# Chunk attention and a multiplicative FFN on one core: the first q and k through the software queue, another order of steps, and three PSUM tiles for the last output

## The chip, the cores and the metric

The kernel runs on one core of one Trainium2 chip. The metric is the device time of one execution in microseconds. The median of four executions before the change is 254.48 us (254.33 to 254.82).

## What is computed

Attention within chunks of 64 positions, then a feed-forward part without a nonlinearity, cut to the core:

```
B, H, S, D = 8, 8, 576, 64            # 9 chunks of 64 in each batch
scores = (q_c @ k_c^T) / sqrt(D)      # 64 x 64 for each chunk and head
attn   = exp(scores - max) / sum
x      = (attn @ v_c), heads side by side      # 4608 tokens x 512
out    = ((x @ w1) * (x @ w2)) @ w3 @ w_out    # w1, w2: 512 x 1024; w3: 1024 x 1024; w_out: 1024 x 512
```

The inputs and the output are fp32.

## The kernel before

The 4608 tokens are cut into 18 "pairs" of 256 tokens, four chunks each. The kernel works in bf16 with sums in fp32. It uses that w3 and w_out follow each other without a nonlinearity: it computes their product once, on the chip, so each pair needs x @ w1, x @ w2, their product, and one further matmul.

All work is written as small steps, and the string ORDER (lines 9 to 37) lists them one after the other. Every instruction is recorded so that each engine keeps this program order. A step that comes earlier in the string therefore stands ahead of all later ones in the queue of its engine, and an engine whose next instruction has to wait stands still. The steps, with p a pair:

- l p loads q, k and v of a pair, q p, k p and v p one of them. i n loads a quarter of the columns of w1 and w2, o loads w_out, h0 and h1 the halves of w3. These loads are issued by GpSimd (POOL) on its software queue and turn fp32 into bf16 on the way (line 91). A load of q or k of a pair writes 1024 rows of 256 bytes; where a pair crosses from one batch into the next, it is split in two. v is loaded in two halves, with rows of 128 bytes.
- q and k of pair 0 are the exception (lines 128 to 134): SP loads them as fp32 into a tile named raw, and ScalarE turns them into bf16.
- T p.0 and T p.1 (VectorE, line 168) transpose q and k in 32x32 blocks. S (TensorE) computes the scores, E (ScalarE, line 184) the exponential, P (TensorE) the product with v, which has a column of ones for the sum. N p.u (VectorE, lines 207 and 209) divides by the sum, X p.u (line 213) transposes the result into xt.
- A p.j and B p.j (TensorE, line 231) multiply xt with quarter j of w1 and of w2. C (ScalarE, line 244) copies A's result out of PSUM, M (VectorE, line 249) multiplies it with B's result into the tile ab.
- V f (VectorE, line 290) transposes an eighth of w3. W m (TensorE) multiplies with w_out, and Z m (ScalarE, line 303) stores that into w3o.
- O p (TensorE, line 260) multiplies ab with w3o, Y p (ScalarE, line 283) copies the result out, and SP stores it. O of the last pair, 17, does this in three parts: first 128 tokens with all 512 columns, then the other 128 tokens with 256 columns and with 256 columns. Each part is copied out (line 276; ScalarE, ScalarE, VectorE) and stored at once.
- D p multiplies zeros, only to keep TensorE busy at the start. Its four numbers are the kind of PSUM tile, the pair, how many, and the columns of each.

All matmuls share one pool of four PSUM tiles of two banks each (lines 81 and 94); a new tile takes the place of the fourth one before it, once that has been read. P takes two tiles. Index u of the tile, or which for A and B, selects the bank.

The 18 pairs are staggered. From pair 5 on, a "slot" takes the attention of a new pair between the matmuls of older pairs: S and P of the new pairs, one O, and the four A and B of another pair.

Of the kernel before, what the change touches and what calls it, by code (L numbers as in the profile page):

```python
# [7 lines left out]

ORDER = """
l0 q1 i0 k1 v1 i1 i2 l2 i3 l3 l4 o h0 h1 l5 D0.0.16.64 T0.0 T0.1 l6 S0 T1.0 E0 P0 D0.1.4.512 T1.1 l7  # L10
N0.0 S1 D1.0.5.512 X0.0 N0.1 X0.1 A0.0 E1 B0.0 C0.0 P1 M0.0 A0.1 N1.0 X1.0 B0.1 C0.1 N1.1 A0.2 X1.1
B0.2 C0.2 M0.1 A1.0 T2.0 B1.0 C1.0 M0.2 A1.1 T2.1 l8 B1.1 C1.1 M1.0 S2 M1.1 A0.3 E2 T3.0 B0.3 C0.3
P2 M0.3 A1.2 N2.0 X2.0 B1.2 C1.2 N2.1 A1.3 X2.1 B1.3 C1.3 M1.2 A2.0 T3.1 l9 B2.0 C2.0 M1.3 S3 T4.0
A2.1 E3 M2.0 B2.1 T4.1 C2.1 P3 l10 M2.1 A2.2 N3.0 B2.2 C2.2 X3.0 A2.3 N3.1 B2.3 X3.1 C2.3 M2.2 S4
M2.3 A3.0 E4 B3.0 C3.0 A3.1 M3.0 B3.1 C3.1 V0 A3.2 M3.1 B3.2 C3.2 V1 A3.3 M3.2 B3.3 C3.3 V2 W0 M3.3
V3 T5.0 W1 Z0 V4 V5 T5.1 W2 Z1 V6 V7 T6.0 P4 l11 Z2 S5 T6.1 W3 E5 N4.0 X4.0 N4.1 X4.1 T7.0 A4.0 Z3
B4.0 T7.1 C4.0 P5 l12 M4.0 S6 N5.0 O0 E6 X5.0 N5.1 X5.1 T8.0 O1 Y0 T8.1 P6 l13 Y1 S7 N6.0 O2 E7 X6.0
N6.1 X6.1 T9.0 T9.1 O3 Y2 A4.1 Y3 B4.1 C4.1 A4.2 M4.1 B4.2 C4.2 A4.3 M4.2 B4.3 C4.3 P7 l14 M4.3 S8
N7.0 O4 E8 X7.0 N7.1 X7.1 T10.0 A5.0 T10.1 Y4 B5.0 C5.0 A5.1 M5.0 B5.1 C5.1 A5.2 M5.1 B5.2 C5.2 A5.3
M5.2 B5.3 C5.3 A6.0 M5.3 B6.0 C6.0 P8 l15 M6.0 S9 N8.0 O5 E9 X8.0 N8.1 X8.1 T11.0 A6.1 T11.1 Y5 B6.1  # L20
C6.1 A6.2 M6.1 B6.2 C6.2 A6.3 M6.2 B6.3 C6.3 P9 l16 M6.3 S10 N9.0 O6 E10 X9.0 N9.1 X9.1 T12.0 A7.0
T12.1 Y6 B7.0 C7.0 A7.1 M7.0 B7.1 C7.1 A7.2 M7.1 B7.2 C7.2 A7.3 M7.2 B7.3 C7.3 P10 l17 M7.3 S11
N10.0 O7 E11 X10.0 N10.1 X10.1 T13.0 A8.0 T13.1 Y7 B8.0 C8.0 A8.1 M8.0 B8.1 C8.1 A8.2 M8.1 B8.2 C8.2
A8.3 M8.2 B8.3 C8.3 P11 M8.3 S12 N11.0 O8 E12 X11.0 N11.1 X11.1 T14.0 A9.0 T14.1 Y8 B9.0 C9.0 A9.1
M9.0 B9.1 C9.1 A9.2 M9.1 B9.2 C9.2 A9.3 M9.2 B9.3 C9.3 P12 M9.3 S13 N12.0 O9 E13 X12.0 N12.1 X12.1
T15.0 A10.0 T15.1 Y9 B10.0 C10.0 A10.1 M10.0 B10.1 C10.1 A10.2 M10.1 B10.2 C10.2 A10.3 M10.2 B10.3
C10.3 P13 M10.3 S14 N13.0 O10 E14 X13.0 N13.1 X13.1 T16.0 A11.0 T16.1 Y10 B11.0 C11.0 A11.1 M11.0
B11.1 C11.1 A11.2 M11.1 B11.2 C11.2 A11.3 M11.2 B11.3 C11.3 P14 M11.3 S15 N14.0 O11 E15 X14.0 N14.1
X14.1 T17.0 A12.0 T17.1 Y11 B12.0 C12.0 A12.1 M12.0 B12.1 C12.1 A12.2 M12.1 B12.2 C12.2 A12.3 M12.2
B12.3 C12.3 P15 M12.3 S16 N15.0 O12 E16 X15.0 N15.1 X15.1 A13.0 Y12 B13.0 C13.0 A13.1 M13.0 B13.1  # L30
C13.1 A13.2 M13.1 B13.2 C13.2 A13.3 M13.2 B13.3 C13.3 P16 M13.3 S17 N16.0 O13 E17 X16.0 N16.1 X16.1
A14.0 Y13 B14.0 C14.0 A14.1 M14.0 B14.1 C14.1 A14.2 M14.1 B14.2 C14.2 A14.3 M14.2 B14.3 C14.3 P17
M14.3 A15.0 N17.0 X17.0 B15.0 C15.0 N17.1 O14 X17.1 M15.0 A15.1 Y14 B15.1 C15.1 A15.2 M15.1 B15.2
C15.2 A15.3 M15.2 B15.3 C15.3 A16.0 M15.3 B16.0 C16.0 O15 M16.0 A16.1 Y15 B16.1 C16.1 A16.2 M16.1
B16.2 C16.2 A16.3 M16.2 B16.3 C16.3 A17.0 M16.3 B17.0 C17.0 O16 M17.0 A17.1 Y16 B17.1 C17.1 A17.2
M17.1 B17.2 C17.2 A17.3 M17.2 B17.3 C17.3 M17.3 O17 Y17
"""


# [1 line left out]
def kernel(  # L41
# [45 lines left out]
    def mm(*a, **kw):
        return inorder(nc.tensor.matmul(*a, **kw))  # L88
# [173 lines left out]

    def do_O(p):
        ps_t[p] = psum("o_ps")
        if p < NP - 1:
# [4 lines left out]

        t = ps_t[p]
        o_sb = msb.tile([P, 2, DM], f32, tag="o_sb", name="o_sb")
        for u, n0, n1, copy in ((0, 0, DM, nc.scalar.copy), (1, 0, DM // 2, nc.scalar.copy),
                                (1, DM // 2, DM, nc.vector.tensor_copy)):
# [1 line left out]
            inorder(copy(o_sb[:, u, n0:n1], t[:, u, n0:n1]))  # L276
# [80 lines left out]
```

The softmax here doesn't subtract the row's maximum and nothing guards it: scores larger than these inputs give would overflow.

## Time and profile before

| what | value |
|---|---|
| median of four executions | 254.48 us |
| the profiled execution | 254.91 us |
| its span, from the first to the last instruction | 253.1 us |
| mean granted TensorE clock | 1.000 |
| first product of x with w1 (A0.0) | 18.22 us |
| first O (O0) | 71.55 us |
| last product | 249.9 us |
| HBM read, written | 38.80 MB, 9.44 MB |

Times within the profile count from the start of the span. In the page's table of busy times each engine has its busy time, its share of the span and its number of instructions. PE is TensorE's products, PEld its loading of weights, which runs beside them; DVE is VectorE, ACT ScalarE, POOL GpSimd. A row of digits shows the busy share, in tenths, in 40 equal slices of the span. A line of the list of waits reads: the engine and line that waited, what it waited for, the total in us, how often, the longest. A line of the timeline reads: start, us taken by the group, engine, line, operation, output<-input, size, count, and in brackets the idle time before it with what ended it. Nearly all matmuls have line 88, a helper's, so they are told apart by their tiles and their place in the order.

### The profile page before, as it was taken

Reading aid. Unit: us, or ns where it says so; the run is one execution under the profiler, and the core shown is the slowest. Engines: PE = TensorE matmul, PEld = TensorE weight load, DVE = VectorE, ACT = ScalarE, POOL = GpSimd, SP = SyncE. Lnnn points to the kernel's source line nnn. Section 1 sums busy time; section 2 is a strip of 40 time slices with the busy share of each in tenths; the row PEclk is TensorE's granted clock in tenths of the full one; section 3 lists DMA queues with packets and bytes.
Section 4 is the critical chain, followed back from the end, with each engine's and each line's share of the span. In section 5 each row is a group of like instructions: output and inputs, shape, how many; then the busy total and the mean of one; then the engine's idle time right before and its main releaser. Section 6 shows DMA issues by size and latency. Waiting matters only on the chain.

```text
span 253.1 us, 8382 instructions
## 1 busy us (share of the span) xinstructions
PE 234.5 (93%) x3841; PEld 170.2 (67%) x3841; DVE 156.0 (62%) x233; ACT 86.1 (34%) x116; POOL 82.7 (33%) x110
## 2 busy tenths in 40 slices
PE   1389989999899999999999999999999999999993
PEld 1247878854555577767868686868686868678662
DVE  1566799599996357486766758584945455432230
ACT  3312414432333343243333243343334332323321
POOL 8757875557974568544020000000000000000000
PEclk9999999999999999999999999999999999999999
DMA  8999999999999999999944020202021120102022
GB/s 176 182 184 177 182 175 202 196 183 169 173 170 214 229 249 167 206 164 143 182 38 98 3 83 4 85 3 85 3 83 39 51 76 9 60 25 84 0 85 83
DMA packets 89763, 29.90 MB, mean 118 GB/s; under 512 B 73728, under 2 KB 85248, under 8 KB 89728
## 3 DMA queue, kind: packets, MB, share of 16 engines
q0 software_dynamic: 82592, 18.88, 80.2%
q1 hardware_dynamic: 7136, 10.49, 11.8%
q8 instruction: 30, 0.49, 0.8%
q14 instruction: 5, 0.04, 0.0%
HBM read 38.80 MB, written 9.44 MB: 191 GB/s over the span
## 4 chain that ended last, share of the span: by engine, by line
PE 65%; DMA 14%; DVE 9%; POOL 4%; issue 3%; ACT 3%; DVEq 0%; POOLq 0%
PE ab_ps L88 39%; PE o_ps L88 25%; DMA w<-in_moe_w_dram 11%; DVE ab L249 4%; DMA vbuf<-in_v_dram 3%; DVE w3T L290 3%; ACT a_sb L244 3%; POOL w L91 1%; DVE qkT L168 1%; POOL vbuf L91 1%; POOL qk L91 1%; PE pv L88 1%; POOL wo L91 1%; PE s_ps L88 1%; DVE xt L213 1%
## 5 line engine op out<-in xcount | busy, mean ns | idle before, releaser
L88 PE MATMUL ab_ps<-xt,w 128*128 128x256 bf16 x1136 | 128.0, 273 | 1.9 <-DVE xt L213 1.9
L88 PEld LDWEIGHTS <-w 128*128 128x128 bf16 x1152 | 112.0, 98 | 19.6 <-DVE xt L213 2.9
L249 DVE TENSOR_TENSOR ab<-a_sb,ab_ps 128x512 bf16<-128x512 f32 x71 | 48.1, 679 | 72.1 <-ACT a_sb L244 72.1
L244 ACT COPY a_sb<-ab_ps 128x512 f32<-128x512 f32 x71 | 41.6, 585 | 79.9 <-PE ab_ps L88 78.7
L88 PE MATMUL o_ps<-w3o,ab 128*128 128x512 bf16 (+1 forms) x296 | 65.3, 373 | 2.5 <-ACT o_sb L276 1.1
L88 PEld LDWEIGHTS <-ab 128*128 128x128 bf16 x296 | 28.6, 97 | 33.2 <-issue 1.6
L168 DVE STREAM_TRANSPOSE qkT<-qk 128x1024 bf16<-128x1024 bf16 x36 | 45.0, 1284 | 9.3 <-ACT qk L133 5.1
L91 POOL DMA_DIRECT2D vbuf<-in_v_dram x40 | 33.9, 853 | 32.8 <-PE pv L88 16.9
L283 ACT COPY o_sb<-o_ps 128x1024 f32<-128x1024 f32 x17 | 17.2, 1012 | 45.8 <-PE o_ps L88 42.9
L213 DVE STREAM_TRANSPOSE xt<-xn 128x512 bf16<-128x512 bf16 x36 | 25.6, 711 | 1.2
L209 DVE TENSOR_TENSOR xn<-pv,rc 128x512 bf16<-128x512 f32 x36 | 24.9, 691 | 1.2
L91 POOL DMA_DIRECT2D qk<-in_q_dram x23 | 18.1, 792 | 6.4 <-DMA qk<-in_k_dram 2.5
L184 ACT ACTIVATE e<-s_ps 128x1024 bf16<-128x1024 f32 x16 | 16.4, 1023 | 9.4 <-PE s_ps L88 9.1
L91 POOL DMA_DIRECT2D qk<-in_k_dram x23 | 18.0, 787 | 3.7 <-DMA w<-in_moe_w_dram 1.8
L88 PEld LDWEIGHTS <-qkT 32*64 32x64 bf16 x1152 | 11.5, 111 | 11.2 <-DVE qkT L168 9.6
L88 PE MATMUL w_ps<-wo,w3T 128*128 128x512 bf16 x64 | 14.2, 379 | 0.0
L88 PEld LDWEIGHTS <-e 64*32 64x32 bf16 x1152 | 10.1, 90 | 5.5 <-issue 3.6
L88 PE MATMUL pv<-vbuf,e 64*32 64x65 bf16 x1152 | 12.7, 197 | 1.1 <-ACT e L184 1.1
L91 POOL DMA_DIRECT2D w<-in_moe_w_dram x16 | 11.1, 695 | 4.6 <-DMA wo<-in_moe_w_out_dram 2.4
L88 PE MATMUL s_ps<-qkT 32*64 32x64 bf16 x1024 | 11.5, 193 | 0.5 <-issue 0.5
L88 PEld LDWEIGHTS <-w3T 128*128 128x128 bf16 x64 | 6.2, 98 | 7.1
L290 DVE STREAM_TRANSPOSE w3T<-w 128x1024 bf16<-128x1024 bf16 x8 | 9.6, 1213 | 1.0 <-DMA w<-in_moe_w_dram 1.0
(20 smaller groups left out, 33.3 us busy)
## 6 DMA issues: line engine op xcount, KB each, us to landing
out_dram<-o_sb SPq DMA_DIRECT2D x17, 512.0 KB, 4.3
vbuf<-in_v_dram POOLq DMA_DIRECT2D x32, 128.0 KB, 6.8
w<-in_moe_w_dram POOLq DMA_DIRECT2D x16, 256.0 KB, 9.8
qk<-in_q_dram POOLq DMA_DIRECT2D x11, 256.0 KB, 7.4
qk<-in_k_dram POOLq DMA_DIRECT2D x11, 256.0 KB, 8.3
wo<-in_moe_w_out_dram POOLq DMA_DIRECT2D x4, 256.0 KB, 6.9
qk<-in_q_dram POOLq DMA_DIRECT2D x4, 192.0 KB, 9.0
qk<-in_k_dram POOLq DMA_DIRECT2D x4, 192.0 KB, 8.9
```

The costliest lines, as they stand in the source:

```text
L88: return inorder(nc.tensor.matmul(*a, **kw))
L91: return inorder(nc.gpsimd.dma_start(dst, src))
L168: inorder(nc.vector.transpose(qkT_t[p][:, s].rearrange("p e h (y t) -> p h t e y", t=2), qk_t[p][:, s].rearrange("p h (t e y) -> p h t e y ...
L184: inorder(nc.scalar.activation(e_t[p][:].rearrange("p u h q -> p u (h q)"), s_t.pop(p)[:], Exp, scale=scale, bias=0.0))
L209: inorder(nc.vector.tensor_mul(xn_t[p, u][:], pv[:, :, :, 0:D], rc.to_broadcast([P, 2, 4, D])))
L213: inorder(nc.vector.transpose(xt[:, :, t0:t0 + UT].rearrange("p o (m y) -> p m o y", y=BL), xn_t.pop((p, u))[:].rearrange("p r (c n) (z o) ...
L244: inorder(nc.scalar.copy(a_t[p, j][:], ps_t[p, j][:, 0, :]))
L249: inorder(nc.vector.tensor_mul(ab_t[p][:, 2 * j:2 * j + 2, :].rearrange("p j t -> p (j t)"), a_t.pop((p, j))[:], ps_t.pop((p, j))[:, 1, :]))
L283: inorder(nc.scalar.copy(o_sb[:], ps_t.pop(p)[:]))
L290: inorder(nc.vector.transpose(w3T_t[f][:].rearrange("p k (f y) -> p f k y", y=BL), w3[:, NB * f:NB * (f + 1), :].rearrange("p f (k x) -> p ...
```

## The change

The change has three parts.

1. The exception for pair 0 goes. Its q and k are loaded by GpSimd on the software queue like all others. ORDER begins with l0 and l1, so q, k and v of pairs 0 and 1 are loaded ahead of the first w1 and w2.
2. ORDER is another one. The steps are the same except for the numbers of D and for which loads are written apart (q2, k2 and v2 in place of q1, k1 and v1). In the slots from pair 5 on, S stands ahead of an A and B of the next pair, and O after these instead of before. P4 and the first A of pair 4 come between the W steps; M of an older product stands ahead of the second X of a pair.
3. O of pair 17 takes a new PSUM tile for each of its three parts.

The order up to O0 before and after, one slot, and the code:

```diff
-l0 q1 i0 k1 v1 i1 i2 l2 i3 l3 l4 o h0 h1 l5 D0.0.16.64 T0.0 T0.1 l6 S0 T1.0 E0 P0 D0.1.4.512 T1.1 l7
-N0.0 S1 D1.0.5.512 X0.0 N0.1 X0.1 A0.0 E1 B0.0 C0.0 P1 M0.0 A0.1 N1.0 X1.0 B0.1 C0.1 N1.1 A0.2 X1.1
-B0.2 C0.2 M0.1 A1.0 T2.0 B1.0 C1.0 M0.2 A1.1 T2.1 l8 B1.1 C1.1 M1.0 S2 M1.1 A0.3 E2 T3.0 B0.3 C0.3
-P2 M0.3 A1.2 N2.0 X2.0 B1.2 C1.2 N2.1 A1.3 X2.1 B1.3 C1.3 M1.2 A2.0 T3.1 l9 B2.0 C2.0 M1.3 S3 T4.0
-A2.1 E3 M2.0 B2.1 T4.1 C2.1 P3 l10 M2.1 A2.2 N3.0 B2.2 C2.2 X3.0 A2.3 N3.1 B2.3 X3.1 C2.3 M2.2 S4
-M2.3 A3.0 E4 B3.0 C3.0 A3.1 M3.0 B3.1 C3.1 V0 A3.2 M3.1 B3.2 C3.2 V1 A3.3 M3.2 B3.3 C3.3 V2 W0 M3.3
-V3 T5.0 W1 Z0 V4 V5 T5.1 W2 Z1 V6 V7 T6.0 P4 l11 Z2 S5 T6.1 W3 E5 N4.0 X4.0 N4.1 X4.1 T7.0 A4.0 Z3
-B4.0 T7.1 C4.0 P5 l12 M4.0 S6 N5.0 O0 E6 X5.0 N5.1 X5.1 T8.0 O1 Y0 T8.1 P6 l13 Y1 S7 N6.0 O2 E7 X6.0
...
-A8.3 M8.2 B8.3 C8.3 P11 M8.3 S12 N11.0 O8 E12 X11.0 N11.1 X11.1 T14.0 A9.0 T14.1 Y8 B9.0 C9.0 A9.1
...
+l0 l1 i0 i1 i2 q2 k2 i3 v2 l3 l4 o h0 l5 h1 D0.0.24.64 T0.0 T0.1 l6 S0 E0 T1.0 P0 D0.1.3.512 T1.1 l7
+S1 D1.0.6.512 N0.0 X0.0 N0.1 X0.1 A0.0 E1 B0.0 C0.0 P1 M0.0 A0.1 N1.0 B0.1 X1.0 C0.1 N1.1 A0.2 M0.1
+B0.2 C0.2 X1.1 M0.2 A1.0 T2.0 B1.0 C1.0 T2.1 l8 A1.1 B1.1 C1.1 M1.0 S2 M1.1 A0.3 E2 B0.3 C0.3 A1.2
+M0.3 B1.2 T3.0 C1.2 P2 M1.2 A1.3 N2.0 B1.3 X2.0 C1.3 N2.1 M1.3 X2.1 T3.1 l9 A2.0 B2.0 T4.0 C2.0 S3
+M2.0 A2.1 E3 T4.1 B2.1 C2.1 P3 l10 M2.1 A2.2 N3.0 B2.2 X3.0 C2.2 N3.1 A2.3 M2.2 B2.3 C2.3 X3.1 S4
+M2.3 A3.0 E4 B3.0 C3.0 A3.1 M3.0 B3.1 V0 C3.1 A3.2 M3.1 B3.2 C3.2 V1 P4 M3.2 A3.3 N4.0 B3.3 C3.3
+X4.0 W0 N4.1 M3.3 X4.1 V2 V3 A4.0 Z0 B4.0 T5.0 C4.0 W1 M4.0 V4 V5 A4.1 T5.1 l11 Z1 B4.1 C4.1 V6 S5
+A4.2 M4.1 E5 V7 B4.2 C4.2 W2 T6.0 M4.2 T6.1 T7.0 P5 l12 Z2 S6 N5.0 A4.3 E6 X5.0 B4.3 N5.1 C4.3 W3
+X5.1 M4.3 T7.1 T8.0 A5.0 Z3 T8.1 B5.0 C5.0 O0 M5.0 P6 l13 Y0 S7 N6.0 A5.1 E7 X6.0 B5.1 N6.1 C5.1 O1
...
+M10.2 B10.3 C10.3 P13 M10.3 S14 N13.0 A11.0 E14 X13.0 B11.0 N13.1 C11.0 O10 X13.1 M11.0 T16.0 T16.1
...
-            if p == 0:
-
-                raw = io.tile([P, H, 2 * D], f32, tag="raw", name="raw")
-                inorder(nc.sync.dma_start(
-                    raw[:], (q, k)[s][0, :, 0:4 * CH, :].rearrange("h (p t) d -> p h (t d)", t=2)))
-                inorder(nc.scalar.copy(qk_t[p][:, s], raw[:]))
-                continue
...
-    def mm_o(p, u, n0, n1):
+    def mm_o(dst, p, u, n0, n1):
         for ki in range(FO):
-            mm(ps_t[p][:, u, n0:n1], lhsT=ab_t[p][:, ki, u * UT:(u + 1) * UT],
+            mm(dst, lhsT=ab_t[p][:, ki, u * UT:(u + 1) * UT],
                rhs=w3o[:, ki, n0:n1], start=(ki == 0), stop=(ki == FO - 1))
 
     def do_O(p):
-        ps_t[p] = psum("o_ps")
         if p < NP - 1:
+            ps_t[p] = psum("o_ps")
             for u in range(2):
-                mm_o(p, u, 0, DM)
+                mm_o(ps_t[p][:, u, :], p, u, 0, DM)
             del ab_t[p]
             return
 
-        t = ps_t[p]
         o_sb = msb.tile([P, 2, DM], f32, tag="o_sb", name="o_sb")
         for u, n0, n1, copy in ((0, 0, DM, nc.scalar.copy), (1, 0, DM // 2, nc.scalar.copy),
                                 (1, DM // 2, DM, nc.vector.tensor_copy)):
-            mm_o(p, u, n0, n1)
-            inorder(copy(o_sb[:, u, n0:n1], t[:, u, n0:n1]))
+            t = psum("o_ps")
+            mm_o(t[:, 0, 0:n1 - n0], p, u, n0, n1)
+            inorder(copy(o_sb[:, u, n0:n1], t[:, 0, 0:n1 - n0]))
             store(p, u, u + 1, n0, n1, o_sb)
```

More of the change, by code (lines that the diff above doesn't have):

```diff
@@ L15 @@
-M2.3 A3.0 E4 B3.0 C3.0 A3.1 M3.0 B3.1 C3.1 V0 A3.2 M3.1 B3.2 C3.2 V1 A3.3 M3.2 B3.3 C3.3 V2 W0 M3.3
-V3 T5.0 W1 Z0 V4 V5 T5.1 W2 Z1 V6 V7 T6.0 P4 l11 Z2 S5 T6.1 W3 E5 N4.0 X4.0 N4.1 X4.1 T7.0 A4.0 Z3
-B4.0 T7.1 C4.0 P5 l12 M4.0 S6 N5.0 O0 E6 X5.0 N5.1 X5.1 T8.0 O1 Y0 T8.1 P6 l13 Y1 S7 N6.0 O2 E7 X6.0
-N6.1 X6.1 T9.0 T9.1 O3 Y2 A4.1 Y3 B4.1 C4.1 A4.2 M4.1 B4.2 C4.2 A4.3 M4.2 B4.3 C4.3 P7 l14 M4.3 S8
-N7.0 O4 E8 X7.0 N7.1 X7.1 T10.0 A5.0 T10.1 Y4 B5.0 C5.0 A5.1 M5.0 B5.1 C5.1 A5.2 M5.1 B5.2 C5.2 A5.3
@@ L20 @@
[L20 to L23, printed above, removed]
-A8.3 M8.2 B8.3 C8.3 P11 M8.3 S12 N11.0 O8 E12 X11.0 N11.1 X11.1 T14.0 A9.0 T14.1 Y8 B9.0 C9.0 A9.1
@@ L25 @@
[L25 to L35, printed above, removed]
@@ L36 @@
-M17.1 B17.2 C17.2 A17.3 M17.2 B17.3 C17.3 M17.3 O17 Y17
+l0 l1 i0 i1 i2 q2 k2 i3 v2 l3 l4 o h0 l5 h1 D0.0.24.64 T0.0 T0.1 l6 S0 E0 T1.0 P0 D0.1.3.512 T1.1 l7
[3 more added lines that the diff above has]
+M2.0 A2.1 E3 T4.1 B2.1 C2.1 P3 l10 M2.1 A2.2 N3.0 B2.2 X3.0 C2.2 N3.1 A2.3 M2.2 B2.3 C2.3 X3.1 S4
@@ new lines @@
+M2.3 A3.0 E4 B3.0 C3.0 A3.1 M3.0 B3.1 V0 C3.1 A3.2 M3.1 B3.2 C3.2 V1 P4 M3.2 A3.3 N4.0 B3.3 C3.3
+X4.0 W0 N4.1 M3.3 X4.1 V2 V3 A4.0 Z0 B4.0 T5.0 C4.0 W1 M4.0 V4 V5 A4.1 T5.1 l11 Z1 B4.1 C4.1 V6 S5
+A4.2 M4.1 E5 V7 B4.2 C4.2 W2 T6.0 M4.2 T6.1 T7.0 P5 l12 Z2 S6 N5.0 A4.3 E6 X5.0 B4.3 N5.1 C4.3 W3
+X5.1 M4.3 T7.1 T8.0 A5.0 Z3 T8.1 B5.0 C5.0 O0 M5.0 P6 l13 Y0 S7 N6.0 A5.1 E7 X6.0 B5.1 N6.1 C5.1 O1
+X6.1 M5.1 T9.0 T9.1 P7 l14 Y1 S8 N7.0 A5.2 E8 X7.0 B5.2 N7.1 C5.2 O2 X7.1 M5.2 T10.0 T10.1 O3 Y2 O4
+Y3 A5.3 Y4 B5.3 C5.3 P8 l15 M5.3 S9 N8.0 A6.0 E9 X8.0 B6.0 N8.1 C6.0 O5 X8.1 M6.0 T11.0 T11.1 A6.1
@@ new lines @@
+Y5 B6.1 C6.1 A6.2 M6.1 B6.2 C6.2 A6.3 M6.2 B6.3 C6.3 P9 l16 M6.3 S10 N9.0 A7.0 E10 X9.0 B7.0 N9.1
+C7.0 O6 X9.1 M7.0 T12.0 T12.1 A7.1 Y6 B7.1 C7.1 A7.2 M7.1 B7.2 C7.2 A7.3 M7.2 B7.3 C7.3 P10 l17 M7.3
+S11 N10.0 A8.0 E11 X10.0 B8.0 N10.1 C8.0 O7 X10.1 M8.0 T13.0 T13.1 A8.1 Y7 B8.1 C8.1 A8.2 M8.1 B8.2
+C8.2 A8.3 M8.2 B8.3 C8.3 A9.0 M8.3 B9.0 C9.0 P11 M9.0 S12 N11.0 A9.1 E12 X11.0 B9.1 N11.1 C9.1 O8
+X11.1 M9.1 T14.0 T14.1 A9.2 Y8 B9.2 C9.2 A9.3 M9.2 B9.3 C9.3 P12 M9.3 S13 N12.0 A10.0 E13 X12.0
+B10.0 N12.1 C10.0 O9 X12.1 M10.0 T15.0 T15.1 A10.1 Y9 B10.1 C10.1 A10.2 M10.1 B10.2 C10.2 A10.3
@@ new lines @@
+M10.2 B10.3 C10.3 P13 M10.3 S14 N13.0 A11.0 E14 X13.0 B11.0 N13.1 C11.0 O10 X13.1 M11.0 T16.0 T16.1
+A11.1 Y10 B11.1 C11.1 A11.2 M11.1 B11.2 C11.2 A11.3 M11.2 B11.3 C11.3 P14 M11.3 S15 N14.0 A12.0 E15
+X14.0 B12.0 N14.1 C12.0 O11 X14.1 M12.0 T17.0 T17.1 A12.1 Y11 B12.1 C12.1 A12.2 M12.1 B12.2 C12.2
+A12.3 M12.2 B12.3 C12.3 P15 M12.3 S16 N15.0 A13.0 E16 X15.0 B13.0 N15.1 C13.0 O12 X15.1 M13.0 A13.1
+Y12 B13.1 C13.1 A13.2 M13.1 B13.2 C13.2 A13.3 M13.2 B13.3 C13.3 P16 M13.3 S17 N16.0 A14.0 E17 X16.0
@@ L37 @@
+B14.0 N16.1 C14.0 O13 X16.1 M14.0 A14.1 Y13 B14.1 C14.1 A14.2 M14.1 B14.2 C14.2 A14.3 M14.2 B14.3
+C14.3 P17 M14.3 A15.0 N17.0 B15.0 X17.0 C15.0 N17.1 O14 M15.0 X17.1 A15.1 Y14 B15.1 C15.1 A15.2
+M15.1 B15.2 C15.2 A15.3 M15.2 B15.3 C15.3 A16.0 M15.3 B16.0 C16.0 O15 M16.0 A16.1 Y15 B16.1 C16.1
+A16.2 M16.1 B16.2 C16.2 A16.3 M16.2 B16.3 C16.3 A17.0 M16.3 B17.0 C17.0 O16 M17.0 A17.1 Y16 B17.1
+C17.1 A17.2 M17.1 B17.2 C17.2 A17.3 M17.2 B17.3 C17.3 M17.3 O17 Y17
 """
```

## The prediction

> **What bounds the kernel now.** I read the page's busy shares first, then the list of TensorE's own waits, then the timeline at the two ends and around each wait, and last the DMA view of short stretches.
>
> ```profile
> PE 234.5 (93%) x3841; PEld 170.2 (67%) x3841; DVE 156.0 (62%) x233; ACT 86.1 (34%) x116; POOL 82.7 (33%) x110
> DMA  8999999999999999999944020202021120102022
> ...
> PE z_ps L88 <- DVE qkT L168: 8.1, 2, 7.1
> PE ab_ps L88 <- DVE xt L213: 1.9, 3, 0.9
> ...
> PE o_ps L88 <- ACT o_sb L276: 1.1, 2, 0.7
> ```
>
> TensorE sets the time: where it isn't waiting, it works. So an edit is worth what it takes from TensorE's gaps, or what it shortens behind the last product. The DMA row is full up to about 125 us: early on everything hangs on the order in which loads leave the queue. The waits add up to little beyond the start: 8.1 us before the first scores, 1.9 us for xt, 1.1 us at the end (columns: total us, times, longest). The timeline (start, us, engine, instructions; in brackets the idle time before and what ended it) shows the two xt waits that count, and what came before the first of them:
>
> ```profile
> 30.87 1.34 DVE L168 STREAM_TRANSPOSE qkT<-qk 128x1024 bf16<-128x1024 bf16 x1 [1.14 <-DMA qk<-in_q_dram]
> ...
> 35.20 0.71 DVE L213 STREAM_TRANSPOSE xt<-xn 128x512 bf16<-128x512 bf16 x1
> ...
> 35.97 1.92 PE L88 MATMUL ab_ps<-xt,w 128*128 128x256 bf16 x16 [0.85 <-DVE xt L213]
> ...
> 68.24 1.92 PE L88 MATMUL ab_ps<-xt,w 128*128 128x256 bf16 x16 [0.69 <-DVE xt L213]
> ...
> 247.34 1.03 PE L88 MATMUL o_ps<-w3o,ab 128*128 128x256 bf16 x8 [0.67 <-ACT o_sb L276]
> ...
> 248.83 1.03 PE L88 MATMUL o_ps<-w3o,ab 128*128 128x256 bf16 x8 [0.46 <-ACT o_sb L276]
> ```
>
> By their places in the order, these are T3.0 at 30.87, X2.1 at 35.20, A2.0 at 35.97, A4.0 at 68.24 and two parts of O17. T3.0 waited for q of pair 3, and VectorE runs in order, so N2.0, X2.0, N2.1 and X2.1 stood behind it, and A2.0 behind X2.1. That chain, not the first scores, sets when the kernel's long run of products begins.
>
> **What the skill says.** "DMA: Bandwidth & Descriptors", section "Issuing engines are not separate DMA queues", says that loads from SP and from GpSimd end on the same 16 DMA engines; only issue time is saved. The trace agrees: pair 0's raw loads fill all DMA engines until about 5.9 us, and the first v load, issued on POOL at 1.24 us, has its first packets only in the 5.5-6.0 stretch. "PSUM — Partial Sum Buffer", section "Terms", makes the bank the unit that two engines may not share. Parts one and two of O17 lie in different banks (u is the bank), and still part two started 0.05 us after the copy of part one: the wait belongs to the tile. "TensorE: Matmul & The Clock Gate", section "What's actually happening", says the array drops to half clock after an idle window of about 3.4 us. The trace has both speeds: five 512-column fills at 16.11 us took 0.42 us each, those of W 0.216 us.
>
> **First q,k by the software queue.** Removed: two SP loads and two ScalarE casts (1.04 us each). Added: two POOL loads at the head. TensorE loses nothing in S0 that matters; what matters is how this moves every later load. From the DMA view of stretches: 725 packets of 256 bytes per us (12 to 13 us), so a q or k load of 1024 packets takes 1.41 us, two 2.82. Before, the software queue had done 738 packets by 6.5 us at 1218 per us, so it flowed as if from 5.9 us. After, q0 is first. Its issue is at 1.24 us; at 129.32 us a load's first packets came 1.5 us after issue, which gives 2.75. The raw loads on a cold chip needed from 1.85 to 2.9 us to reach full rate; I add 0.65 and take 3.4. Then v0 follows at 3.4 + 2.8 = 6.2 us, 0.3 later than before. Bounds: 3.0 (0.1 early) and 5.9 (the trace can't say when the software queue could have begun; 2.8 late). All loads up to q3 are the same set in both orders, only permuted, and the queue never runs dry, so q3 lands 0.3 us later: 30.82 becomes 31.1.
>
> **The order up to A2.0.** T3.0 still stands ahead of N2.0 on VectorE. Before, from T3.0's start to A2.0 it took 35.97 - 30.87 = 5.10 us, with one product (M0.3) in between. After, M1.2 and M1.3 stand there: one more, 0.57 us from start to next start (32.11 to 32.68). So A2.0 starts at 31.17 + 5.67 = 36.84, 0.87 later. TensorE's own work would have allowed it earlier: w2's third part landed at 21.66 by the chain of waits, now + 0.3, and from B0.2's end at about 22.9 the five remaining A/B pairs of pairs 0 and 1 (1.75 each), S2 and P2 (0.64 each) and small gaps end near 33.4. So the gain of the earlier start (k1, now ahead of w1, lands near 11.4 instead of 13.7; T1.1, S1 and six fills later A0.0 starts near 16.4 instead of 18.22) turns into a wait of about 3.4 us before A2.0. The same pairs lie ahead of A2.0 in both orders, so nothing is banked.
>
> **From A2.0 to O0.** S3, P3 and S4 are covered as before. M2.2 now precedes X3.1. Before, X3.1 ended at 44.95 and A3.0 started at 45.17, 0.22 to spare; one product (0.57) more makes it about 0.3 late. Then W0 stands between P4 and A4.0: VectorE needs M3.2, N4, X4, M3.3 (some 4.5 us after P4), TensorE has A3.3 and W0 (1.75 + 3.45 = 5.2): the 0.69 wait at A4.0 goes. The eight w3 transposes are spread over A4.0 to A4.2; T5.1 ends about as TensorE reaches S5 (T5.0, M4.0, V4, V5, T5.1 follow V3), so 0 to 0.5 us there; I take 0. h1's last load, issued at 43.83 and by the median of such loads landed 9.8 later, moves behind l5 (2.82 + 2 x 0.84 = 4.5 us) to about 58.4; V4, at 56.95 before, comes near 60.8, so it is covered.
>
> **The steady slots.** Before, O stands after S and waits for the M of the previous product block:
>
> ```profile
> 129.19 0.71 PE L88 MATMUL s_ps<-qkT 32*64 32x64 bf16 x64
> ...
> 129.29 0.69 DVE L249 TENSOR_TENSOR ab<-a_sb,ab_ps 128x512 bf16<-128x512 f32 x1 [1.06 <-ACT a_sb L244]
> ...
> 129.83 3.32 PEld L88 LDWEIGHTS <-ab 128*128 128x128 bf16 x16
> ...
> 130.03 3.61 PE L88 MATMUL o_ps<-w3o,ab 128*128 128x512 bf16 x16
> ```
>
> The weights were loaded at 129.83, M ended at 129.98, the product came 0.05 later: 0.2 us lost in each of nine slots. After, an A stands there. But PSUM has four tiles, and behind S they are held by the last A, two pv and the s tile: the new A needs the tile that the same M frees. So the 0.2 stays, moved from O to A. O, now behind A and B, needs what N frees, long done. I count 0; bounds -1.8 and +0.3.
>
> **The last output.** Three tiles: part two needs no copy of part one (0.67), part three none of part two (0.46). The tiles wanted are freed by Y16, M17.1 and M17.2, all done. TensorE's end, the VectorE copy and the last store move up by 1.13 us, and nothing else is on that path. The two ScalarE copies then lie beside TensorE's parts two and three.
>
> **Sum.** 0.87 + 0.3 - 0.69 - 1.13 = -0.65 us against the profiled execution's 254.91 (span 253.1 and 1.8 around it): 254.26. That execution lies 0.43 above the median 254.48, so 253.8.
>
> **Rivals.**
> (1) Slower: the software queue's cold start is late. Every load waits with it, and q3, T3.0, X2.1, A2.0 follow one for one. It decides from a flow start of 3.4 + 0.65 = 4.05 us on. At 5.9 it costs 2.5 more: 254.48 - 0.65 + 2.5 = 256.3. For it: no software packet shows before 5.5 us. Against: until then the raw loads kept the DMA engines busy, and later loads flow after 1.5 us.
> (2) Slower too: the 3.4 us wait before A2.0 drops the clock. A2.0, B2.0 and what follows for one window run at half speed, about 1.7 us more: 255.5. Against: my wait is just at the window's length, and the window must be idle from end to end.
> (3) Faster: the slots' waits do go, because the PSUM tile of A is another than I read: 253.83 - 1.8 = 252.0. Against: in the lines above the loaded weights show that the O product itself waited, as it would for a tile.
> (4) No change: S5 and X3.1 each cost 0.3 more: 254.4.
>
> **How the numbers follow.** Forecast 0.46 (its own range 253.2 to 254.5), (1) 0.26, (2) 0.10, (3) 0.10, (4) 0.08. About 0.2% (0.5 us) is what a measurement can tell from no change. Faster: 0.37 of the forecast and (3), 0.47. Same: 0.09 of the forecast, (4) and 0.03 of (1), 0.20. Slower: 0.33. The range runs from 252.8 to 256.4: it leaves out most of (3) and a little at the upper end.
>
> **What would show it.** Right: A2.0 near 36.8 after a TensorE gap of some 3 us, named by xt, with T3.0 waiting for q3 near 31; no wait at A4.0; O products in slots with no gap, and 0.2 us at the A behind S; no wait for ScalarE in O17, which takes 1.1 us less. Wrong: q3 landing past 32, software packets first seen after 4 us, A2.0 and B2.0 taking far over the 1.92 us of before, or slots shorter than the 12.0 us of before (118.03 to 130.03).

## The result and the profile after

| | before | after |
|---|---|---|
| median of the executions run side by side (46 and 28) | 254.77 us | 254.97 us |
| lowest, highest | 254.31, 255.12 | 254.50, 256.22 |
| profiled execution, its span | 254.91, 253.1 us | 255.00, 253.2 us |

The ratio of after to before is 1.0017, with a 95% interval from 1.0009 to 1.0025: by the ratio 0.4 us slower, less than the 0.5 us that count here as a change. The forecast was 0.65 us faster. The 28 executions of the changed kernel form two sets: 16 with a mean granted TensorE clock of 1.000 (254.50 to 255.15, median 254.62) and 12 with 0.991 to 0.993 (255.45 to 256.22, median 255.77). The kernel before ran again beside the experiments, 27, 31 and 42 times with its clock on record, and has 0.996 or more in all that are used here. One of those executions (312.38 us) and one with fills ahead of A2.0 (282.98 us) fell into a slower state of the chip and are left out throughout. So there are two things to explain: why the set at full clock comes out level instead of 0.65 faster, and why the clock falls in the other.

The page's table of busy times and the row of DMA shares, after:

```profile
PE 234.3 (93%) x3849; PEld 169.9 (67%) x3849; DVE 154.9 (61%) x233; ACT 84.0 (33%) x114; POOL 84.5 (33%) x112
...
DMA  7999999999999999999936102202020202022022
```

TensorE does the same work as before, and the DMA engines are full as long. The change is in the gaps. The list of TensorE's waits, after (what it waited for, total us, times, longest):

```profile
PE z_ps L88 <- DVE qkT L161: 6.1, 2, 5.9
PE ab_ps L88 <- DVE xt L206: 2.8, 2, 2.7
...
PE w_ps L88 <- issue: 0.9, 1, 0.9
...
PE ab_ps L88 <- DVE ab L242: 0.5, 1, 0.5
PE s_ps L88 <- ACT o_sb L276: 0.4, 1, 0.4
```

The two waits of O17 are gone, and so are 2 us of the wait for the first scores. But xt has grown from 1.9 to 2.8, in one piece of 2.7, and the last three lines are new. The timeline after shows where each lies (VectorE's lines first, since they cause the long one):

```profile
30.70 0.69 DVE L242 TENSOR_TENSOR ab<-a_sb,ab_ps 128x512 bf16<-128x512 f32 x1 [2.12 <-ACT a_sb L237]
31.39 1.32 DVE L161 STREAM_TRANSPOSE qkT<-qk 128x1024 bf16<-128x1024 bf16 x1
...
36.18 0.70 DVE L206 STREAM_TRANSPOSE xt<-xn 128x512 bf16<-128x512 bf16 x1
...
36.94 1.92 PE L88 MATMUL ab_ps<-xt,w 128*128 128x256 bf16 x16 [2.66 <-DVE xt L206]
...
46.37 5.41 PE L88 MATMUL ab_ps<-xt,w 128*128 128x256 bf16 x48 [0.16 <-DVE xt L206]
...
77.01 1.25 PE L88 MATMUL w_ps<-wo,w3T 128*128 128x512 bf16 x5 [0.88 <-issue]
...
105.23 1.01 ACT L276 COPY o_sb<-o_ps 128x1024 f32<-128x1024 f32 x1 [4.08 <-DMA out_dram<-o_sb]
...
106.29 0.70 PE L88 MATMUL s_ps<-qkT 32*64 32x64 bf16 x64 [0.40 <-ACT o_sb L276]
...
107.50 1.91 PE L88 MATMUL ab_ps<-xt,w 128*128 128x256 bf16 x16 [0.51 <-DVE ab L242]
...
118.66 0.71 PE L88 MATMUL s_ps<-qkT 32*64 32x64 bf16 x64
119.50 1.91 PE L88 MATMUL ab_ps<-xt,w 128*128 128x256 bf16 x16
121.24 3.62 PE L88 MATMUL o_ps<-w3o,ab 128*128 128x512 bf16 x16
...
245.96 3.92 PE L88 MATMUL o_ps<-w3o,ab 128*128 128x512 bf16 x24
```

In order: M0.3 and T3.0; X2.1; A2.0; A3.0; the last five products of W3; Y4; S9 and A6.0 behind it; S, A and O of a steady slot; O17. A4.0 follows W0 and has no gap.

The matching places before: A3.0, the rest of S9 behind its gap, and the first part of O17.

```profile
45.18 7.16 PE L88 MATMUL ab_ps<-xt,w 128*128 128x256 bf16 x64
...
107.41 0.43 PE L88 MATMUL s_ps<-qkT 32*64 32x64 bf16 x29 [0.49 <-issue]
...
244.49 2.17 PE L88 MATMUL o_ps<-w3o,ab 128*128 128x512 bf16 x8
```

Set against the profile before, place by place (start later or earlier, us):

| place | before | after | adds |
|---|---|---|---|
| A2.0 starts | 35.97 | 36.94 | +0.97 |
| A3.0 starts | 45.17 | 46.37 | +0.23 more |
| gap at A4.0 | 0.69 | none | -0.69 |
| "issue" gap in W3 | none | 0.88 | +0.88 |
| "issue" gap in S9 | 0.49 | none | -0.49 |
| S9 and A6.0, beyond a slot's usual 0.2 | none | 0.40 + 0.51 - 0.20 | +0.71 |
| O17, start to its last product's end | 5.37 | 3.92 | -1.45 |

The sum is +0.16; the last products end at 249.86 and 249.88 and the spans differ by 0.1, so some 0.1 us lies at places not listed. The changed kernel reaches O17 1.47 us late (245.96 against 244.49) and wins 1.45 back there.

### The profile page after: what moved, and what is told of

Same layout as the page of the kernel before. It is cut to its first block, busy times and chain, and to the rows that moved or that the text cites. A ratio compares the mean times of both kernels' runs of the same rounds, so it can differ in the third digit from the quotient of the medians.

```text
span 253.2 us, 8386 instructions
## 1 busy us (share of the span) xinstructions
PE 234.3 (93%) x3849; PEld 169.9 (67%) x3849; DVE 154.9 (61%) x233; ACT 84.0 (33%) x114; POOL 84.5 (33%) x112
## 4 chain that ended last, share of the span: by engine, by line
PE 74%; DVE 8%; DMA 7%; POOL 4%; ACT 3%; issue 2%; ACTq 0%; POOLq 0%
PE ab_ps L88 45%; PE o_ps L88 21%; PE w_ps L88 6%; DMA w<-in_moe_w_dram 4%; DVE ab L242 4%; ACT a_sb L237 3%; DMA out_dram<-o_sb 3%; PE s_ps L88 2%; POOL qk L91 1%; POOL vbuf L91 1%; PE pv L88 1%; DVE qkT L161 1%; POOL w L91 1%; DVE xn L202 1%; DVE xt L206 1%
## 5 line engine op out<-in xcount | busy, mean ns | idle before, releaser
L88 PE MATMUL ab_ps<-xt,w 128*128 128x256 bf16 x1136 | 130.8, 273 | 5.1 <-DVE xt L206 2.8
L91 POOL DMA_DIRECT2D qk<-in_q_dram x24 | 19.1, 797 | 6.5 <-DMA qk<-in_k_dram 2.0
L91 POOL DMA_DIRECT2D qk<-in_k_dram x24 | 19.0, 799 | 3.1 <-DMA w<-in_moe_w_dram 2.3
```

## The experiments

Times are medians; each ratio is to the kernel before on the same chip, whose median was 254.80 beside the first four runs, 254.54 beside the next four and 254.51 beside the last three. Where no other base is named, the edit is made to the changed kernel. A fill is a product with zeros, a step D.

**The last output alone.** The kernel before with nothing but part 3 of the change.

```diff
     def do_O(p):
-        ps_t[p] = psum("o_ps")
         if p < NP - 1:
+            ps_t[p] = psum("o_ps")
...
+            t = psum("o_ps")
+            mm_o(t[:, 0, 0:n1 - n0], p, u, n0, n1)
+            inorder(copy(o_sb[:, u, n0:n1], t[:, 0, 0:n1 - n0]))
```

> The kernel before with part 3 of the change alone. My theory (the last output gains, other places give it back): TensorE's two waits for ScalarE in O17 (0.67 and 0.46 us) go and nothing else moves, so 1.0 to 1.1 us less than before, about 253.7. Rival (the last output gains nothing on the clock, because the stores set the end): the end of the last product moves up, the time stays within 0.3 us of before.

Measured: 252.96 us, ratio 0.9933 (0.9922 to 0.9945), 1.84 us less. Its timeline has

```profile
243.85 3.92 PE L88 MATMUL o_ps<-w3o,ab 128*128 128x512 bf16 x23
```

The three parts run as one group. From 5.37 to 3.92 is 1.45 us, not the 1.13 that the two waits come to: broken into three, the products themselves took 2.17 + 1.03 + 1.03 = 4.23 us, in one group 3.92. The other 0.39 of the 1.84 is less plain. The 0.49 us "issue" gap in S9 is absent from this profile, though TensorE's instructions come in the same order. What such a gap waits for is seen under "More fills at the head". So part 3 is worth more than forecast, and the rest of the change must cost some 2 us.

**A third store buffer.** Y writes into o_sb, of which there are two.

```diff
-o_sb = msb.tile([P, 2, DM], f32, tag="o_sb", name="o_sb")
+o_sb = msb.tile([P, 2, DM], f32, tag="o_sb", bufs=3, name="o_sb")
```

> The changed kernel with three instead of two buffers for the outputs on their way to the store. My theory: Y4 waited for the store of O2, which took 7.4 us to land, and C5.3, M5.3, S9 and A6.0 stood behind it; with a third buffer the gaps of 0.40 us before S9 and 0.51 us before A6.0 shrink to the 0.2 us of every slot, so 0.7 us less than the changed kernel, 254.2 to 254.3. Rival: TensorE would have waited there for another thing anyway (a product block's M): the time stays within 0.2 us of the changed kernel's 254.97.

Measured: 255.51 us, ratio 1.0033 (1.0020 to 1.0046). Four of the five executions have a clock of 0.991 to 0.993; the fifth, at full clock, took 255.05. The gaps at S9 and A6.0 are gone, so the store was their cause. But the time didn't fall, since this run shows something else. Its timeline, and its windows for TensorE (stretch, us, busy and count, granted clock, DMA share, GB/s):

```profile
36.86 2.82 PE L88 MATMUL ab_ps<-xt,w 128*128 128x256 bf16 x16 [2.59 <-DVE xt L206]
...
47.78 5.41 PE L88 MATMUL ab_ps<-xt,w 128*128 128x256 bf16 x48 [0.16 <-DVE xt L206]
...
78.35 1.25 PE L88 MATMUL w_ps<-wo,w3T 128*128 128x512 bf16 x5 [0.81 <-issue]
```

```profile
37.00:40.00 3.00, 3.00 (x44) 0.62 1.57 191
40.00:44.00 4.00, 4.00 (x139) 0.86 1.30 204
```

A2.0 starts where it did, but its 16 products take 2.82 us instead of 1.92, at 0.62 of the clock, and A3.0 comes at 47.78 instead of 46.37. In the same two stretches of the changed kernel's profile the clock is 1.00. Followed more closely, the granted clock is 0.50 from 37.72 to 41.13, for 3.41 us, and 1.00 on both sides of that. So it looks as if the wait before A2.0 lowers the clock in some executions, which would be rival (2); the fills below test it. It costs 1.49 us from A2.0 to A3.0 here (10.92 against 9.43); over the 28 executions of the changed kernel the two sets lie 1.15 us apart.

**More fills at the head.** To see whether the "issue" gap belongs to W3 or to a count of instructions.

```diff
-D0.0.24.64
+D0.0.64.64
```

> The changed kernel with 64 instead of 24 zero products at the very start, where TensorE is idle until about 8.5 us; they take about 2.6 us more and lie within that. Only the count of TensorE's instructions ahead of each step changes. My theory: the gap of 0.88 us in the middle of W3, which waits for nothing that the profile shows, comes from the fetching of TensorE's instructions while the DMA engines are full, so it depends on where the blocks of instructions end; with 40 more pairs of instructions ahead it leaves W3 and is either gone (about 254.1) or at another place. Rival: the gap belongs to W3 itself (its weights from the transposes of w3, or its PSUM tile): it stays at W3 with 0.9 us, and the time stays at 254.97.

Measured: 258.16 us, ratio 1.0131 (1.0114 to 1.0149). Four of its five executions have a clock of 0.967 to 0.973; the fifth, at 0.999, took 258.65. Its timeline:

```profile
14.92 0.69 PE L88 MATMUL z_ps<-qkT 32*64 32x64 bf16 x36 [1.25 <-issue]
...
96.64 10.09 PE L88 MATMUL o_ps<-w3o,ab 128*128 128x512 bf16 x46 [1.45 <-issue]
```

W3 has no gap now. There are two others of the kind, in S1 and among O2 to O4. Forty small products ahead moved them, so the place follows from how many instructions stand ahead. (The profiled execution also has a wait of 2.59 us at A2.0 and a fall of the clock behind it. Why the fifth execution, close to full clock, is no faster isn't known.)

In the changed kernel's DMA view the instruction queue has 30 packets, 0.49 MB in all, 16 KB each; 3849 products with as many weight loads make 7698 instructions, 257 for each packet. Counted through ORDER, the "issue" gaps of this document's profiles lie behind product 223, 734, 1244, 1372, 1627 or 1756, which are 128 products (256 instructions) or a multiple of that apart, to within four. The DMA records of the traces hold the packets of that queue too, and each gap ends shortly after one of them:

| profile | gap in | packet ends | TensorE goes on | after |
|---|---|---|---|---|
| before | S9 | 105.95 | 107.41 | 1.46 |
| changed | W3 | 75.76 | 77.01 | 1.25 |
| more fills | S1 | 13.61 | 14.92 | 1.31 |
| more fills | O2 | 95.25 | 96.64 | 1.39 |

The gaps of 0.4 us and more of the other profiles end 1.2 to 1.6 us after a packet as well. So TensorE waits there for its next block of instructions. With part 3 alone the packet at S9 ended at 104.83, 1.1 us sooner than before, and there was no gap. That a packet comes late because the DMA engines are full is argued only: all gaps of 0.4 us and more lie before 108 us, and the DMA row is full to about 125.

**The first q and k by SP.** Part 1 undone, the rest kept.

```diff
+            if p == 0:
+
+                raw = io.tile([P, H, 2 * D], f32, tag="raw", name="raw")
...
+                inorder(nc.scalar.copy(qk_t[p][:, s], raw[:]))
+                continue
```

> The changed kernel with part 1 undone: q and k of pair 0 by SP and ScalarE again, in the new order. My theory: in the changed kernel the software queue stands 0.5 to 0.6 us behind that of before from q3 on, and the products of pairs 0 and 1 and T3.0 follow the loads; so A2.0 comes 0.5 us earlier (36.4 instead of 36.94) and the time is 0.5 us less, about 254.5. Rival: A2.0 is set by VectorE's own chain from M0.3 to X2.1 and by the order of the steps, not by the loads: A2.0 stays at 36.9 and the time at 254.97.

Measured: 255.59 us, ratio 1.0021 (1.0007 to 1.0036), in two sets again: eight executions at full clock (254.12 to 254.77, median 254.22) and fourteen at 0.991 to 0.993 (255.34 to 256.40). At full clock it lies about 0.4 below the changed kernel, but more of its executions lose the clock. The profiled one shows the wait and the slow products behind it:

```profile
37.25 3.02 PE L88 MATMUL ab_ps<-xt,w 128*128 128x256 bf16 x16 [2.60 <-DVE xt L213]
```

The long wait thus isn't due to the software queue; it comes with the order. A2.0 was expected at 36.4 and starts at 37.25, though q of pair 3 landed at about 30.5, 0.8 us sooner than in the changed kernel: T3.0 starts at 31.69, directly behind M0.3, and waits for no load. That is what the rival of this experiment said: VectorE's own chain sets A2.0.

**Fills ahead of A2.0**, to keep TensorE busy in that wait, first alone and then with the third buffer.

```diff
-l9 A2.0 B2.0
+l9 D1.2.10.512 A2.0 B2.0
```

> The changed kernel with ten zero products of 512 columns (2.2 us at full clock) put on TensorE right before A2.0, into the 2.66 us in which it waits for xt; A2.0 can still start when X2.1 ends. My theory: in part of the executions the wait lets the granted clock fall, and A2.0 and what follows run slower for about 3 us (the two sets among the changed kernel's executions: 254.5 to 255.15 at a granted clock of 1.0, and 255.45 to 256.2 at 0.991 to 0.993). With the array kept busy all executions have a clock of 1.0 and lie at 254.5 to 254.8. Rival: the lower clock has nothing to do with that wait: the fills leave the two sets as they are, or add up to 0.3 us by their instructions.

> The same with three instead of two output buffers as well. My theory: without the clock's fall the gain of the third buffer shows: 0.5 to 0.7 us less than with the fills alone, about 254.0. Rival: the wait for the store is replaced by the next thing at the same place: no difference to the fills alone.

Measured: 255.40 (ratio 1.0034, 1.0021 to 1.0046) and 255.09 us (1.0022, 1.0016 to 1.0029). No execution in either ratio has a clock below 0.998. So it is the idle stretch that lowers the clock, and ten products prevent it. The times are still above both what was expected and the changed kernel at full clock, whose ratio to the kernel before would be 0.9994 (254.62 to 254.77). The timeline of the second shows why in part:

```profile
36.89 1.91 PE L88 MATMUL z_ps<-xt,w 128*128 128x256 bf16 x16 [0.47 <-DVE xt L206]
...
44.75 1.59 PE L88 MATMUL ab_ps<-xt,w 128*128 128x256 bf16 x13 [0.66 <-issue]
...
75.39 3.41 PE L88 MATMUL w_ps<-wo,w3T 128*128 128x512 bf16 x15 [0.89 <-issue]
```

A2.0 is no earlier and keeps its 1.91 us. A new "issue" gap of 0.66 stands in A2.3. The one in W3 comes after the first product of 16 instead of after the eleventh: ten products earlier, for ten fills more. That is the clearest sign that the gap belongs to a place in the instruction stream. The third buffer takes 0.3 us off, where 0.5 to 0.7 were expected, and the two intervals overlap; in the timeline the waits at S9 and A6.0 are gone.

**The head of before, the rest of after.** The kernel before up to S4, with SP's loads, then the new order; three tiles for O17; three store buffers.

```diff
-l0 l1 i0 i1 i2 q2 k2 i3 v2 l3 l4 o h0 l5 h1 D0.0.24.64 T0.0 T0.1 l6 S0 E0 T1.0 P0 D0.1.3.512 T1.1 l7
...
+l0 q1 i0 k1 v1 i1 i2 l2 i3 l3 l4 o h0 h1 l5 D0.0.16.64 T0.0 T0.1 l6 S0 T1.0 E0 P0 D0.1.4.512 T1.1 l7
...
```

> The order of before up to S4 (with q and k of pair 0 by SP), the changed order from S4 on, three tiles for the last output and three output buffers. My theory: the loss of the new order lies up to A3.0 (46.37 against 45.17) and in the store's wait, its gain is the wait of 0.69 us at A4.0 and the last output: so A3.0 at 45.2, no wait at A4.0, and with the durations of the two profiles 45.17 + 33.47 + 165.4 + 7.24 + 1.8 = 253.1 us; 252.2 if the gap of 0.88 us in W3 goes as the instructions move. Rival: the loss of the changed kernel lies in the slots and not at the head: 254.0 or more.

Measured: 253.18 us, ratio 0.9943 (0.9925 to 0.9961), all at full clock; A2.0 starts at 35.88 and A3.0 at 45.09. By the ratios (0.9943 against 0.9994) that is 1.3 us below the changed kernel at full clock, and A3.0, 1.28 sooner, has nearly all of it. It still has gaps of 0.34 at A3.3, 0.35 at S5 and 0.41 ("issue") in S7. So the loss sits mostly ahead of S4; how much of the rest the third buffer adds isn't told apart here.

**The software queue alone.** The kernel before with nothing but part 1.

```diff
-            if p == 0:
-
-                raw = io.tile([P, H, 2 * D], f32, tag="raw", name="raw")
...
-                continue
```

> The kernel before with part 1 of the change alone: q and k of pair 0 by the software queue ahead of v of pair 0, the order of before. My theory: the software queue stands 0.6 us behind from there on; T3.0 waits for q of pair 3, so A2.0 comes 0.6 us later (36.6 instead of 35.97) and the time is 0.6 us more, 255.4. Rival: scores start 0.8 us earlier (8.5 instead of 9.36), the later loads have slack, and the time is the same or up to 0.5 us less.

Measured: 255.57 us, ratio 1.0044 (1.0031 to 1.0057), 1.1 us slower. Its timeline:

```profile
8.60 1.07 PE L88 MATMUL z_ps<-qkT 32*64 32x64 bf16 x64 [6.37 <-DVE qkT L161]
...
16.32 1.07 PE L88 MATMUL z_ps<-qkT 32*64 32x64 bf16 x64 [2.96 <-DVE qkT L161]
...
37.33 1.92 PE L88 MATMUL ab_ps<-xt,w 128*128 128x256 bf16 x16 [0.15 <-DVE xt L206]
```

S0 is early, and then S1 waits 2.96 us for pair 1, whose k stands behind w1 in that order. T3.0 starts at 31.55, behind M1.1 and about when q of pair 3 lands. A2.0 comes 1.36 us later than before with hardly a gap: here TensorE itself is late. The new order, which loads pair 1 first, brings A2.0 back to 36.94.

**Products behind X.** M1.3 behind X2.1 and M2.2 behind X3.1, to take one product out of the chain ahead of A2.0.

```diff
-N2.1 M1.3 X2.1 T3.1
+N2.1 X2.1 M1.3 T3.1
...
-A2.3 M2.2 B2.3 C2.3 X3.1 S4 M2.3
+A2.3 B2.3 C2.3 X3.1 M2.2 S4 M2.3
```

> The changed kernel with two products put back behind the transpose that TensorE waits for: M1.3 behind X2.1 and M2.2 behind X3.1. My theory: VectorE's queue sets A2.0 and A3.0, one product (0.57 us) each: A2.0 at 36.4 instead of 36.94, no wait before A3.0; the wait before A2.0 is 2.1 instead of 2.66 us, so fewer executions fall to the clock of 0.992, and those at 1.0 lie 0.7 us under the changed kernel's 254.6, about 253.9. Rival: the load of q of pair 3 or TensorE's own P2 sets A2.0: it stays at 36.9.

Measured: 255.22 us, ratio 1.0024 (1.0017 to 1.0032), in two sets again: nine of 21 executions at full clock, median 254.87, and twelve at 0.991 to 0.993. So neither expectation came in: as many fall, and those at full clock gain nothing. The wait at A3.0 is gone, but A2.0 starts at 36.74, only 0.2 earlier, after a gap of 2.46. In this profile T3.0 started at 31.64 (31.39 in the changed kernel), 0.25 us of it waiting for q of pair 3, and took back part of the gain, and S5 now waits 0.36 us for qkT. The product in the chain was not the main matter.

**P2 early.** P2 ahead of A1.2, T3.0 behind X2.1, what follows one block later.

```diff
-A1.2 M0.3 B1.2 T3.0 C1.2 P2 M1.2 A1.3 N2.0 B1.3 X2.0 C1.3 N2.1 M1.3 X2.1 T3.1 l9 A2.0
+P2 M0.3 A1.2 N2.0 B1.2 X2.0 C1.2 N2.1 A1.3 X2.1 B1.3 C1.3 T3.0 M1.2 l9 A2.0
...
```

> The changed kernel with P2 ahead of A1.2 (as before the change), T3.0 behind X2.1, and S3 and P3 one product block later. My theory: T3.0, waiting for the loads, and the late P2 are what holds X2.1; so X2.1 ends about 34.7 and A2.0 starts at 35.0 or earlier with under 0.5 us of wait, every execution has a clock of 1.0, and A3.0 starts near 45.2 (46.37 in the changed kernel), with a wait of 1.1 us ahead of it: about 253.4. Rival: v of pair 2, now behind w1_3 and w2_3, comes too late for the early P2: TensorE waits there instead and A2.0 stays at 36.9; about 254.6.

Measured: 254.91 us, ratio 1.0016 (1.0010 to 1.0023), every execution at a clock of 0.997 or more. Its timeline:

```profile
33.83 0.71 DVE L206 STREAM_TRANSPOSE xt<-xn 128x512 bf16<-128x512 bf16 x1
...
34.60 3.67 PE L88 MATMUL ab_ps<-xt,w 128*128 128x256 bf16 x32 [0.33 <-DVE xt L206]
...
41.66 0.32 PE L88 MATMUL pv<-vbuf,e 64*32 64x65 bf16 x32 [0.66 <-DVE ab L242]
...
44.34 0.50 PE L88 MATMUL ab_ps<-xt,w 128*128 128x256 bf16 x3 [0.84 <-issue]
```

A2.0 starts 2.3 us earlier than in the changed kernel, and the clock holds. Three steps of VectorE that stood ahead of X2.1 now stand behind it: T3.0, M1.2 and M1.3, 1.22 + 0.57 + 0.60 = 2.39 us by their durations. They are what held A2.0 up, and the early P2 lets N2 and X2 go before them. But A3.0 starts only 0.96 earlier, and the forecast of 253.4 failed: 0.66 is lost in P3, whose tiles wait for a product on VectorE, 0.84 to "issue" in A2.3, and 0.36 at S5, gaps that the changed kernel does not have. Those in W3 (1.01) and at S9 and A6.0 (0.78) are about as long as there.

**A version that beats both.** The kernel before with part 3 and one piece of part 2: P4 two W steps earlier, and S5 behind W3, so that N4 and X4 are done when A4.0 is reached.

```diff
-V4 V5 T5.1 W2 Z1 V6 V7 T6.0 P4 l11 Z2 S5 T6.1 W3 E5 N4.0 X4.0 N4.1 X4.1 T7.0 A4.0
+V4 V5 P4 l11 V6 W2 Z1 V7 N4.0 X4.0 N4.1 X4.1 T5.1 W3 Z2 T6.0 S5 Z3 E5 T6.1 A4.0
```

> The kernel before with three tiles for the last output (as in the run with part 3 alone) and P4 two w3 products earlier, so that N4 and X4 are done ahead of A4.0; S5 behind W3. My theory: the wait of 0.69 us before A4.0 goes and nothing takes its place: 0.6 to 0.7 us under the run with part 3 alone, 252.3. Rival: VectorE is full there, so the wait moves to W3 or S5: 252.8 to 253.2.

Measured: 252.20 us, ratio 0.9921 (0.9897 to 0.9946). From the list of TensorE's waits in its profile:

```profile
PE z_ps L88 <- DVE qkT L168: 8.0, 2, 7.0
...
PE ab_ps L88 <- DVE xt L213: 0.9, 2, 0.6
```

The 0.9 are A1.0 (0.33) and A2.0 (0.61). A4.0 no longer waits, and no "issue" gap stands in the list. This is 2.3 us below the kernel before and, by the ratios, 2.4 below the changed one. That it also beats part 3 alone isn't shown: the ratios (0.9921 and 0.9933) differ by 0.3 us, where 0.6 to 0.7 were expected, and their intervals overlap.

## Why the prediction was wrong

**First q,k by the software queue: right in direction, too small.** The flow was taken to start as if from 3.4 us. By packets (265 between 3 and 4 us, 699 in the next) it started as from 3.6. So q3 landed at 31.36, 0.54 later than before and not 0.3; in three other profiles with these loads it landed between 31.1 and 31.7, and with part 1 alone at about 31.5. Rival (1) had its point of decision at 4.05 and did not come in. Part 1 alone costs 1.1 us in the old order, but most of that is S1 waiting behind w1, which the new order avoids.

**A2.0: the number right, the path only in part.** 36.84 was forecast, 36.94 measured. N2, X2 and one more M behind T3.0 held X2.1 as described: 5.55 us from T3.0 to A2.0, where 5.67 were forecast. But T3.0 did not wait for q3. It starts at 31.39, just as M0.3 ends, with no wait in the line; q3 landed at about the same moment. With q3 0.8 us sooner ("The first q and k by SP") T3.0 stood behind M0.3 all the same. Two chains that end within 0.3 us of each other set it, so the near agreement of the number is partly luck. The wait was put at 3.4 and measured 2.66, because TensorE finished A1.3 at 34.28 instead of 33.4.

**"Against: my wait is just at the window's length, and the window must be idle from end to end" failed.** With this sentence the prediction gave the fall of the clock a chance of 0.10. A lower clock came in 12 of 28 executions, and in the three profiles that show the fall the wait was 2.59 or 2.60 us, shorter than the window of about 3.4 us that the Trainium skill gives in "TensorE: Matmul & The Clock Gate", section "What's actually happening". The half clock and the length of the window agree with the traces (0.50 for 3.41 us); that the window must be idle throughout does not. In these three profiles (third buffer, more fills, first q and k by SP) TensorE was idle for 2.55 to 2.60 of the 3.41 us up to the fall and busy for the rest. The same section of the Trainium skill says that the window is free-running, which is to say that it does not start anew with the kernel. The traces fit: in all three the fall comes 20.48 us, six times 3.41, after the clock's first rise, so the windows run on from there and the wait does not start a new one. The changed kernel's profile kept its clock through 2.66 us of wait; counted the same way from its rise at 14.52, a window ends at 35.00 and cuts that wait into 0.72 and 1.94. In "Products behind X" one ends at 36.06 and cuts the wait of 2.46 into 1.79 and 0.68, and the clock held. So what seems to count is how much of the wait falls into one window. Five profiles agree with that; they do not prove it. The size was near: 1.7 forecast for the fall itself, 1.15 between the sets. In the median it makes 0.35 (254.97 against 254.62).

**A3.0, A4.0 and the slots: right.** A3.0 waits 0.16 where 0.3 were forecast, A4.0 not at all. In the slots the 0.2 us stands at the A behind S (S at 118.66, A at 119.50: 0.84 us, where an A behind an S that waits for nothing comes after 0.64), O follows without a gap, and the period is 12.0 us as before. Rival (3) is out.

**The last output: the mechanism right, the size off.** The term of 1.13 measured 1.45: left out was that the products take 0.31 us longer in three pieces than in one group.

**The sum failed for what it doesn't contain.** At full clock the change was -0.65 by the terms; they measured, in the same places, 0.97 + 0.23 - 0.69 - 1.45 = -0.94. Against this stand +0.71 and +0.88 - 0.49, and the whole comes to +0.16. The step that failed is thus one that the prediction put at nothing: what the new order does to TensorE between A4.0 and the steady slots, beyond the waits that it named.

- The +0.71 is the store of O2. The step "From A2.0 to O0" ends at O0, and "The steady slots" takes its model at 129 us. Between the two the new order puts O2, O3 and O4 with Y2 to Y4 within ten microseconds, while loads still fill the DMA engines. The store of O2, issued at 97.7, takes 7.40 us to land, and with two store buffers Y4 waits for it. So long a landing is no exception there: of the changed kernel's 17 such stores the five issued before 107 us took 5.2 to 7.5, while the median of all is 3.0. The profile before had the same in view, where it did no harm: five stores issued before 100 us took 6.5 to 7.6, and ScalarE waited for one. ScalarE is in order: C5.3 stands behind Y4, M5.3 behind C5.3, and S9 and A6.0 need the PSUM tiles. The third buffer removes the waits at S9 and A6.0: that is shown by the timelines. In the measured times it comes to 0.3 us, with overlapping intervals.
- The +0.88 - 0.49 are blocks of instructions that arrive late. The prediction left out the 0.49 us of the profile before and assumed nothing new of the kind. That its place moves with the number of instructions is shown by the fills, and that TensorE waits for a block by the times of the packets; that full DMA engines hold the packet up is argued. How large a gap will be could not be foreseen from the profile before.

The lines behind the first point: ScalarE's wait for a store in the profile before (total us, times, longest), and the store of O2 in the one after (issued at, us to land).

```profile
ACT o_sb L283 <- DMA out_dram<-o_sb: 2.9, 1, 2.9
...
97.72 7.40 DMA out_dram<-o_sb
```

What stays open: why the packet at S9 came sooner with part 3 alone, and how part 2 would do by itself without the two others, which wasn't run. By difference at full clock, parts 2 and 3 together (254.22) lie 1.3 us above part 3 alone (252.96), so that the new order costs more than it saves. Parts 1 and 2 together cost 0.48 by the prediction's terms (0.87 + 0.3 - 0.69); by the ratios at full clock (0.9994 against 0.9933) they cost some 1.5.

## What to carry to other kernels

A sum over the places that one has looked at is only as good as the stretch that was left out; follow every moved step through the part where the order is irregular, with its copy, its store and the buffer that the store holds. Take a store's time to land from the stretch where the loads run, not from the median of all. An earlier start that ends in a longer wait banks nothing and may cost the clock: count a wait of 2.5 us on TensorE as a risk, not only one of the full window. Test the parts of a mixed change alone: here one part was worth 1.8 us, and the others hid it.

## What was not expected of the hardware

- A wait of 2.59 us on TensorE lowered the granted clock to 0.50 for 3.41 us. A lower clock shows in 12 of 28 executions of the changed kernel, and in none of 21 once ten fills and a third buffer were in.
- TensorE stood 0.4 to 1.45 us with no wait that the lists name, at places 128 products or a multiple apart in its instruction stream, and went on 1.2 to 1.6 us after a 16 KB packet of the instruction queue had ended. 10 or 40 more products ahead moved the places, and not every such place stalls in every kernel.
- 512 KB stores took 5.2 to 7.5 us to land while loads filled the DMA engines (five of them, issued before 107 us), against a median of 3.0 over all 17.
- The software queue's first load was issued at 1.25 us; its first packet came at 2.95, 1.7 us later, and the full flow only as from 3.6. The Trainium skill, "DMA: Bandwidth & Descriptors", section "Latency and other measured facts", gives about 1 us to the first byte on the software queue; at this start the packet took longer, and the flow 2.4 us.
